# Three mask transposes moved from TensorE to a DMA, and a new written-out order, in an attention-and-MLP kernel

## The chip, the core and the metric

One core of a Trainium2 chip runs the whole program in one launch. The metric is device time in microseconds, from the start of the execution to its end. TensorE (PE) multiplies; VectorE (DVE), ScalarE (ACT) and GpSimd (POOL) do the rest; SyncE (SP) issues nearly all DMAs, in program order.

## The reference

Two parts follow one another. The first is block-sparse causal attention, with 4 batches of 8 heads, 768 positions and 64 features; each query sees its own block of 64 keys and the three blocks whose mean key scores highest:

```python
k_rep = k.reshape(B, H, n_blocks, block, D).mean(axis=3)
gate_scores = np.einsum('bhsd,bhnd->bhsn', q, k_rep)
gate_scores = np.where(causal, gate_scores, -1000000000.0)
top_idx = np.argsort(gate_scores, axis=-1)[..., -top_k:]
...   # mask: chosen blocks and the own block, causal inside
scores = np.where(mask, scale * np.matmul(q, k.transpose(0, 1, 3, 2)), -1000000000.0)
...   # softmax, then attn @ v
```

The second takes the attention output as 3072 rows of 512 features through an MLP: up-projection to 2048, gelu in its tanh form, down-projection to 512. Inputs and output are float32.

## The kernel before, in words

*Heads.* Heads are handled two at a time, as 16 pairs, 4 for each batch. Pairs 0 to 3 (batch 0) are handled in two groups g of two pairs and in three thirds c of 256 positions, so that work can begin before all of batch 0 is loaded. Pairs 4 to 15 are handled whole.

*MLP.* Rows go in 12 chunks of 256. For each chunk there are four up tiles (`up`, L957, 16 matmuls of 256 columns in two halves), four gelus (`gelu`, L967) and two row tiles of four down steps (`down`, L993). A chunk needs the transposed attention output `xT` of all four pairs of its batch: chunk 0 needs the first thirds of batch 0, chunk 1 the second thirds. The last chunk's second row tile is cut into 384 and 128 columns.

*Order.* There is no scheduler. A string `ORDER` lists every step by name, and the program issues them in this order; on each engine's queue instructions run strictly in order, each after the semaphores of what it needs. A name may carry an engine (`:a` ACT, `:v` DVE, `:p` POOL) and one of three wide PSUM slots (`@0` to `@2`).

The step names that the text uses:
- `d0`, `dd`, `d`: loads of q, k and v, from SP; the first k loads (`d0.g.t.1`) come from ACT's queue (L372). `lw`, `cw`: loads of the MLP weights and their casts to fp16. `r`: a copy that puts a loaded 256-position part into order for the transposes.
- `t2`, `h2`, `l` (batch 0): transposes of q and k on PE (L464), and the high and low fp16 parts. `hn`, `ln`, then `zqh`, `zkh`, `zql` (L751): the same for pairs 4 to 15, with the transposes done by DMA from SP.
- `s`, `b`: key sums by block. `g` (L794): gate scores. `m` (`select`, L807 to L821): the top three of each row on DVE, which ends in `madd16`, an fp16 tile of 128 positions by 12 half-chunks.
- `mt` (`mask_t`, L830): the mask is transposed by PE, five blocks of 128x128, into the `small` PSUM bank, of which there is one. `mc` (`mask_q`, L839): two copies put its 12 rows per head under the transposed queries, so that the score matmul adds the mask. `c0`, `c1` (L758): copies of the transposed q and k to where the score matmul reads them.
- `k` (scores, L598 and L852), `x` (exponential, L635 and L868), `a` (causal cut on POOL, L648 and L882), `p` (probabilities times v, L662 and L894), `n` (division by the row sum). `ma` (L616): adds the mask in batch 0.
- `xt` with `xc`, or `zx` (L903): the transpose of the attention output into `xT`, by PE or by DMA.
- `u.chunk.tile.half`, `y`, `f.chunk.row.step`, `o` (L1006, copy out of PSUM) and `w` (L1011, write to HBM).
- `dmN`: N units of 128 columns of filler matmuls on zeros (L1032).

What sets the order of work around the change: the one `small` bank is used in turn by key sums, gate scores, masks, some output transposes and at the end by down tiles. Buffers of a tag rotate; the tag `ql` (two buffers) holds the transposed low part of q.

Of the kernel before, what the change touches and what calls it, by code (L numbers as in the profile page):

```python
# [32 lines left out]
s.0.1 mc.1.0:a dm4 l.0.1 k.0.0.0.0@2 k.0.0.1.0@1 ma.0.0.0 x.0.0.0.0 d0.1.1.2 v.1.0.0:p c.par.0
b.0.1 b.1.1 dm16 d0.0.1.2 x.0.0.1.0 a.0.0.1 g.0.1 k.0.1.0.1@0 k.1.0.0.0@2 k.1.0.1.0@1 ma.1.0.0
x.1.0.0.0 a.0.0.0 lw.out.1 x.1.0.1.0 m.0.1 dd.0.2.1 r.0.2.1:a mt.0.1 mc.0.1:v lw.in.4 g.1.1
k.0.1.1.1@2 v.0.0.1:p lw.in.5 ma.0.1.1 x.0.1.1.1 m.1.1 x.0.1.0.1 t2.0.2@1 d0.0.3.2 s.0.2 h2.0.2
a.0.1.0 dm9 v.0.1.1:a lw.in.3 d0.0.2.2 v.1.1.1:a l.0.2 a.1.0.1 v.1.0.1:p k.1.1.1.0@2 mt.1.1
mc.1.1:v v.0.0.0:p k.1.1.0.0@0 ma.1.1.0 x.1.1.1.0 a.0.1.1 p.0.0.0@1 p.0.0.2 p.0.0.3 p.0.0.1 n.0.0
dm22 d0.1.2.2 cw.in.5:v lw.in.1 v.1.1.0:p dd.1.2.0 cw.in.1:v k.1.1.0.1@2 k.1.1.1.1@1 ma.1.1.1
x.1.1.0.0 a.1.0.0 cw.in.4:v p.1.0.0@0 x.1.1.1.1 d.5.1 dd.1.2.1 dm23 v.0.1.0:p lw.out.0 x.1.1.0.1  # L40
r.1.2.0:a xt.0.0 xc.0.0:a lw.in.0 p.1.0.2 cw.in.2:p d.4.0 p.1.0.3 p.1.0.1 n.1.0 k.0.1.0.0@1
k.0.1.1.0@2 ma.0.1.0 x.0.1.0.0 a.1.1.0 p.1.1.0@0 p.1.1.1 xt.1.0 xc.1.0:v a.1.1.1 p.1.1.2 r.1.2.1:v
lw.out.5 x.0.1.1.0 cw.out.5:p d0.1.5.2 p.0.1.0@1 p.0.1.1 p.1.1.3 n.1.1 cw.in.3:v d.4.1 lw.in.6
lw.in.7 cw.out.1:a hn1.5.0:v p.0.1.3 cw.in.6:p cw.in.7:p lw.out.3 p.0.1.2 t2.1.2@2 n.0.1 s.1.2
b.1.2 xt.1.1 u.0.1.0@0 xc.1.1:a u.0.1.1 y.0.1 hn0.4.0:v xt.0.1 xc.0.1:a b.0.2 u.0.2.0@1 u.0.2.1
y.0.2 u.1.2.0@0 u.1.2.1 y.1.2 u.1.1.0@1 u.1.1.1 ln0.4.0:v zql.4.0 lw.out.2 y.1.1 d0.0.5.2
cw.out.0:a cw.in.0:v u.0.0.0@0 u.0.0.1 g.0.2 u.1.0.0@1 u.1.0.1 y.0.0 hn1.4.0:v u.0.3.0@0 m.0.2
cw.out.3:v mt.0.2 u.0.3.1 h2.1.2 l.1.2 y.1.0 dm9 ln1.4.0:v dm24 y.0.3 cw.out.2:v mc.0.2:v
k.0.2.1.0@2 k.0.2.0.0@1 ma.0.2.0 x.0.2.0.0 g.1.2 d.6.0 hn0.6.0:p x.0.2.1.0 k.0.2.0.1@0 k.0.2.1.1@1
zqh.4.0 ma.0.2.1 x.0.2.0.1 x.0.2.1.1 c.ke.0.0:p ln1.5.0:v m.1.2 mt.1.2 k.0.2.1.2@2 mc.1.2:v s.4.0  # L50
b.4.0 k.0.2.0.2@0 c0.4.0.0:a lw.out.6 ma.0.2.2 f.0.0.0 lw.out.4 lw.out.7 x.0.2.1.2 ln0.6.0:v
cw.out.7:v f.0.0.1 x.0.2.0.2 k.1.2.0.0@1 k.1.2.1.0@2 zkh.5.0 ma.1.2.0 x.1.2.1.0 zqh.6.0 cw.out.6:p
x.1.2.0.0 c.ke.0.1:v cw.out.4:p g.4.0 m.4.0 f.0.0.2 d0.0.4.2 v.0.2.0:v f.0.0.3 o.0.0:a d.5.0
k.1.2.0.1@0 k.1.2.1.1@2 ma.1.2.1 d0.1.4.2 f.0.1.0 hn0.5.0:v ln0.5.0:v x.1.2.0.1 a.0.2.0 zkh.4.0
v.0.2.1:p a.0.2.1 f.0.1.1 p.0.2.0@1 p.0.2.1 c.ke.1.0:a x.1.2.1.1 c0.4.0.1:p mt.4.0 d.6.1 v.1.2.1:p
c1.4.0.0:a mc.4.0.0:v c.par.1 p.0.2.3 p.0.2.2 n.0.2 v.1.2.0:a k.1.2.1.2@0 zqh.5.0 k.1.2.0.2@2
ma.1.2.2 f.0.1.2 x.1.2.0.2 f.0.1.3 zql.5.0 c1.4.0.1:v mc.4.0.1:v x.1.2.1.2 s.5.0 b.5.0 o.0.1:v
k.4.0.1@1 k.4.0.2@2 x.4.0.1 d.4.2 d.5.2 c1.5.0.0:v zql.6.0 a.1.2.0 p.1.2.0@0 p.1.2.1 g.5.0 m.5.0
x.4.0.2 c0.5.0.0:v a.1.2.1 p.1.2.3 c.q0.0 k.4.0.0@1 v.4.0:p f.1.0.0 x.4.0.0 xt.0.2 xc.0.2:a
k.4.0.5@2 p.1.2.2 x.4.0.5 k.4.0.3@1 x.4.0.3 a.4.0.3 hn1.6.0:v d.7.1 ln1.6.0:v a.4.0.5 mt.5.0 d.8.0  # L60
mc.5.0.0:v c0.5.0.1:p zkh.6.0 k.4.0.4@2 f.1.0.1 mc.5.0.1:v n.1.2 c0.6.0.1:v x.4.0.4 u.1.3.0@1
u.1.3.1 y.1.3 s.6.0 f.1.0.2 b.6.0 xt.1.2 w.0.0 xc.1.2:v d.7.0 c1.5.0.1:p hn1.7.0:v ln1.7.0:v
c.ke.1.1:p k.5.0.2@0 k.5.0.1@2 x.5.0.2 k.5.0.3@1 g.6.0 m.6.0 f.1.0.3 u.2.0.0@0 o.1.0:v d.8.1
u.2.0.1 d.9.0 x.5.0.3 a.4.0.4 a.4.0.2 a.4.0.0 a.4.0.1 p.4.0.0@1 x.5.0.1 a.5.0.1 hn0.7.0:v zqh.7.0
mt.6.0 mc.6.0.1:v d.6.2 p.4.0.1 w.1.0 mc.6.0.0:v n.4.0 c1.6.0.0:p y.2.0 c0.6.0.0:p k.5.0.4@2
c1.6.0.1:p f.1.1.0 f.1.1.1 ln0.7.0:v x.5.0.4 c.q0.1 hn1.8.0:v ln1.8.0:v k.5.0.5@1 k.6.0.2@0 x.6.0.2
s.7.0 b.7.0 f.1.1.2 v.5.0:v k.5.0.0@2 c0.7.0.1:v hn0.8.0:p x.5.0.5 ln0.8.0:v x.5.0.0 k.6.0.3@0
a.5.0.0 zql.7.0 zkh.7.0 zqh.8.0 s.8.0 f.1.1.3 b.8.0 x.6.0.3 o.1.1:a a.6.0.3 w.1.1 k.6.0.4@1 w.0.1
x.6.0.4 u.2.1.0@2 u.2.2.0@0 u.2.2.1 y.2.2 hn0.9.0:p g.7.0 a.5.0.4 u.2.1.1 c0.7.0.0:v y.2.1
u.2.3.0@1 m.7.0 a.6.0.4 u.2.3.1 mt.7.0 zql.8.0 y.2.3 a.5.0.2 ln0.9.0:v a.5.0.3 a.5.0.5 p.5.0.0@0  # L70
p.5.0.1 mc.7.0.0:v k.6.0.1@2 f.2.0.0 f.2.0.1 x.6.0.1 v.6.0:v d.10.0 a.6.0.1 n.5.0 k.6.0.0@1
k.6.0.5@2 f.2.0.2 c1.7.0.1:v x.6.0.5 a.6.0.5 x.6.0.0 mc.7.0.1:v c1.7.0.0:v k.7.0.5@0 k.7.0.2@2
zkh.8.0 x.7.0.5 c1.8.0.1:p g.8.0 x.7.0.2 hn0.10.0:v m.8.0 d.7.2 a.6.0.0 a.6.0.2 f.2.0.3 o.2.0:a
k.7.0.3@1 x.7.0.3 a.7.0.3 zx.5.0 c0.8.0.0:a k.7.0.0@0 p.6.0.0@2 p.6.0.1 x.7.0.0 mt.8.0 k.7.0.4@1
x.7.0.4 n.6.0 f.2.1.0 mc.8.0.0:v k.7.0.1@0 f.2.1.1 a.7.0.2 a.7.0.4 mc.8.0.1:a zx.4.0 c0.8.0.1:v
c1.8.0.0:v k.8.0.3@1 d.9.1 zqh.9.0 d.10.1 d.8.2 zql.9.0 a.7.0.0 d.11.0 x.7.0.1 a.7.0.1 v.7.0:v
k.8.0.1@2 x.8.0.1 a.7.0.5 x.8.0.3 xt.6.0 xc.6.0:v p.7.0.0@0 p.7.0.1 n.7.0 hn1.9.0:a zkh.9.0
c1.9.0.0:p hn1.10.0:v ln0.10.0:v zql.10.0 f.2.1.2 f.2.1.3 w.2.0 k.8.0.5@2 xt.7.0 x.8.0.5 k.8.0.4@1
xc.7.0:a zqh.10.0 k.8.0.2@0 u.3.3.0@2 u.3.3.1 ln1.9.0:v x.8.0.4 s.9.0 x.8.0.2 a.8.0.2 u.3.2.0@1
u.3.2.1 v.8.0:v u.4.2.0@0 u.4.2.1 b.9.0 g.9.0 ln1.10.0:v d.11.2 zkh.10.0 y.3.3 o.2.1:a y.3.2 y.4.2  # L80
# [1003 lines left out]
```

## Time and profile before

| | |
|---|---|
| runs (3) | 276.27, 277.47 (median), 279.40 us |
| profiled execution | 278.32 us, span 276.6 us, mean granted TensorE clock 0.994 |
| PE busy | 263.3 us (95%) |
| ACT busy | 198.2 us (72%), with table loads |
| DVE, POOL busy | 141.4 us, 86.9 us |
| read from, written to HBM | 27.26 MB, 6.29 MB |

The span runs from the first to the last instruction of the core; the execution's own time is 1.7 us longer. A busy PE counts a matmul from its start to its modelled end, and matmuls overlap, so the work of PE is better read from how far apart the starts of matmuls lie. Idle time of an engine off the critical path costs nothing.

### The profile page before, as it was taken

The numbers are of one execution on the slowest core, as the hardware profiler recorded it, in microseconds if no ns is written. First come the engines' busy times: TensorE is split into PE (matmuls) and PEld (weight loads), VectorE is DVE, ScalarE is ACT, GpSimd is POOL, SyncE is SP. The second block draws the span as 40 slices with busy tenths as digits, with TensorE's granted clock in tenths as the row PEclk, the third lists the DMA queues.
The fourth block names the chain that finished last, engine by engine and source line by source line (L and its number), as shares of the span: only waits on it lengthen the run. The fifth ranks groups of instructions, "written<-read, shape, count | busy, mean of one in ns | idle before, by whom it ended". The sixth has DMA issues, their size and how long they took to land.

```text
span 276.6 us, 6874 instructions
## 1 busy us (share of the span) xinstructions
PE 263.3 (95%) x2785; PEld 183.1 (66%) x2785; DVE 141.4 (51%) x442; ACT 198.2 (72%) x229; POOL 86.9 (31%) x159
## 2 busy tenths in 40 slices
...
GB/s 173 279 329 282 252 270 295 276 170 180 175 248 192 177 199 190 185 200 213 148 212 118 188 119 114 101 135 157 79 7 23 97 0 2 0 76 2 76 92 138
DMA packets 114416, 42.66 MB, mean 154 GB/s; under 512 B 102992, under 2 KB 107344, under 8 KB 114384
## 3 DMA queue, kind: packets, MB, share of 16 engines
...
q14 instruction: 10, 0.08, 0.1%
HBM read 27.26 MB, written 6.29 MB: 121 GB/s over the span
## 4 chain that ended last, share of the span: by engine, by line
PE 70%; DVE 8%; DMA 7%; ACT 7%; issue 4%; POOL 2%; SPq 1%; POOLq 0%; ACTq 0%
PE hps L957 23%; PE ops L993 20%; PE st L852 7%; PE pv L894 4%; DMA io<-in_k_dram 4%; PE pso L993 3%; PE dm L1032 3%; ACT at L868 2%; DMA qhT<-hn 2%; DMA io<-in_q_dram 2%; PE st L598 2%; DVE ln L739 2%; ACT L868 1%; PE pv L662 1%; PE st L616 1%
## 5 line engine op out<-in xcount | busy, mean ns | idle before, releaser
L957 PE MATMUL hps<-xT,w_in 128*128 128x256 f16 x768 | 90.1, 272 | 0.0
L957 PEld LDWEIGHTS <-w_in 128*128 128x128 f16 x768 | 74.0, 98 | 12.5 <-DVE xn L677 0.2
L993 PE MATMUL ops<-w_out,gT 128*128 128x512 f16 (+1 forms) x352 | 81.9, 371 | 0.0
L868 ACT ACTIVATE at<-st 128x1024 f16<-128x1024 f32 (+1 forms) x72 | 62.8, 918 | 11.1 <-PE st L852 10.8
L967 ACT ACTIVATE gT<-hps 128x1024 f16<-128x1024 f32 x48 | 48.1, 1024 | 23.0 <-PE hps L957 22.8
L993 PEld LDWEIGHTS <-gT 128*128 128x128 f16 x400 | 37.0, 97 | 36.2 <-issue 0.5
L882 POOL TENSOR_SCALAR_AFFINE_SELECT at<-at 128x256 f16<-128x256 f16 x72 | 31.1, 451 | 76.4 <-ACT at L868 66.6
L852 PE MATMUL st<-qk 76*128 76x128 f16 (+2 forms) x192 | 35.6, 306 | 0.5 <-ACT at L868 0.5
L739 DVE SCALAR_TENSOR_TENSOR ln<-io,hn 128x768 f16<-128x768 f32 x24 | 25.3, 1059 | 0.3
L635 ACT ACTIVATE at<-st 128x768 f16<-128x768 f32 (+1 forms) x24 | 20.7, 913 | 6.5 <-PE st L616 4.9
L852 PEld LDWEIGHTS <-qk 76*128 76x128 f16 x192 | 16.5, 97 | 10.8 <-issue 0.9
L1006 DVE COPY w_o<-pso 128x512 f32<-128x512 f32 x1 | 0.7, 692 | 36.9 <-PE pso L993 36.9
L894 PEld LDWEIGHTS <-at 128*128 128x128 f16 x504 | 17.1, 97 | 2.5 <-issue 0.6
L894 PE MATMUL pv<-v,at 128*128 128x65 f16 x504 | 17.7, 193 | 0.6 <-POOL v L771 0.6
L1006 ACT COPY osb<-ops 128x512 f32<-128x512 f32 (+1 forms) x13 | 7.3, 562 | 14.8 <-PE ops L993 12.8
L187 POOL TENSOR_SCALAR hn<-io 128x768 f16<-128x768 f32 x6 | 13.0, 2160 | 9.2 <-PE hps L957 5.1
L1032 PE MATMUL dm<-zsrc 128*128 128x512 f16 (+3 forms) x45 | 13.4, 431 | 2.0 <-POOL zsrc L235 2.0
L673 DVE RECIPROCAL zrec<-pv 128x12 f32<-128x12 f32 x12 | 2.8, 232 | 22.6 <-PE pv L894 22.4
L967 ACT ACT_TABLE_LOAD x11 | 14.1, 1283 | 0.2
L839 DVE COPY qk<-mt 12x640 f16<-12x640 f16 x19 | 9.2, 485 | 7.9 <-ACT qk L839 4.3
L648 POOL TENSOR_SCALAR_AFFINE_SELECT at<-at 128x512 f16<-128x512 f16 x12 | 7.8, 661 | 17.3 <-ACT at L635 17.1
L868 ACT ACT_TABLE_LOAD x9 | 11.5, 1283 | 2.2 <-PE st L852 2.0
...
## 6 DMA issues: line engine op xcount, KB each, us to landing
...
out_dram<-osb SPq DMA_DIRECT2D x15, 256.0 KB, 2.5
...
out_dram<-w_o SPq DMA_DIRECT2D x8, 256.0 KB, 2.4
io<-in_v_dram SPq DMA_DIRECT2D x12, 128.0 KB, 6.1
```

Of the source, the lines that this page charges most:

```text
L187: math_on[eng].tensor_scalar(out=out, in0=in_, scalar1=c, scalar2=None, op0=ALU.mult)
L635: nc.scalar.activation(out=ov, in_=iv, func=AF.Exp, bias=0.0, scale=SCALE / (QS * QS))
L739: math_on[eng].scalar_tensor_tensor(out=g.rearrange("p t c -> p (t c)"), in0=IO[p, x].rearrange("p t h d -> p (t h d)"), scalar=QS, in1=U[ ...
L839: copy_on[eng](out=qt[p % 2][hh][64:64 + NBLK, 128:], in_=U["mt", p][64 * hh:64 * hh + NBLK, 0:S - 128])
L852: nc.tensor.matmul(st[:, hh, cb:cb + nq * 128], kt[p % 2][hh][0:64 + NBLK, jc * 128:(jc + 1) * 128], qt[p % 2][hh][0:64 + NBLK, qc * 128:( ...
L868: nc.scalar.activation(out=ov, in_=iv, func=AF.Exp, bias=0.0, scale=SCALE / (QS * QS))
L882: nc.gpsimd.affine_select(out=a, in_=a, compare_op=ALU.is_ge, fill=0.0, base=0, pattern=[[0, 2], [1, 128]], channel_multiplier=-1,)
L894: nc.tensor.matmul(U["pv", p][:, o:o + 65], AT[p, hh, jc, qc], v16[p % NSLOT][:, jc, hh, :], start=(jc == 0), stop=(jc == qc),)
L957: nc.tensor.matmul(hps[:, j * TCH:(j + 1) * TCH], w_in16[:, ci, fi * 128:(fi + 1) * 128], xT[:, ci, t0:t0 + TCH], start=(ci == 0), stop=(c ...
L967: nc.scalar.activation(out=g.rearrange("p a w -> p (a w)"), in_=G["h", ch, dj], func=AF.Gelu_apprx_tanh, bias=0.0, scale=1.0,)
L993: nc.tensor.matmul(G["o", ch, ti][:, a:b], G["g", ch, dj][:, j, row * 128:(row + 1) * 128], w_out16[:, fi, a:b], start=(fi == 0), stop=(fi ...
L1032: nc.tensor.matmul(U["dm"][:, 0:m * 128].rearrange("p (a x) -> p a x", a=m), zsrc, zsrc.unsqueeze(1).to_broadcast([128, m, 128]), start=Tr ...
```

## The change

Two things change. For pairs 13, 14 and 15 the step `mt` becomes `zm`: SP issues one DMA transpose of `madd16` (five blocks of 128x128, the source of the `mt` step) into an SBUF tile of the tag `ql`, and the two `mc` copies read that tile and no longer PSUM. And `ORDER` is another one from its first to its last name. All other steps are the same in kind and number; engines and slots differ.

```diff
+    def mask_dma(p):
+        mt = hd.tile([128, S - 128], FP16, tag="ql", name=f"mt_{p}")
+        nc.sync.dma_start_transpose(
+            out=mt.rearrange("d (t p) -> d t p", p=128),
+            in_=madd16[p % 2][:, 2:2 * NC].rearrange("p a b -> p (a b)"))
+        U["mt", p] = mt
...
-        step(f"mt.{un}", mask_t, p)
+        if p in (13, 14, 15):
+            step(f"zm.{un}", mask_dma, p)
+        else:
+            step(f"mt.{un}", mask_t, p)
```

In the new order all eight up tiles of chunks 0 and 1 stand ahead of the first scores of the third thirds (`k.0.2`); in the old one seven did, and `u.1.3` came after the first scores of pair 4. Pieces of both orders, not adjacent ones:

```diff
  # the opening
-c.m0.1 c.bi c.ident d0.0.1.0 c.e0 d0.1.0.0 c.ident16 dm24 d0.1.0.1 d0.0.0.0 d0.0.0.1 dd.1.1.0
-dd.1.1.1 d0.1.3.2 d0.0.1.1 t2.0.0@0 c.e.2:a c.v.1 d0.1.1.0 d0.1.1.1 c.gate dm4 c.own r.1.1.0:a
+c.par.0 d0.1.1.0 d0.1.0.0 d0.0.1.0 d0.1.0.1 c.m0.1 d0.0.1.1 d0.0.0.0 c.ident c.ident16 d0.0.0.1
+c.e0 c.own dm24 dm11 dd.0.1.1 dm4 d0.1.1.1 t2.1.0@0 dd.0.1.0 c.m0.0 c.gate c.cg c.bd h2.1.0 s.1.0
...
  # u.1.3, now ahead of k.0.2
-x.4.0.4 u.1.3.0@1 u.1.3.1 y.1.3 s.6.0
+u.0.1.0@2 u.0.1.1 y.1.0 y.0.1 u.1.3.0@1 u.1.3.1 d.5.0 hn0.5.0:p k.0.2.0.0@0 y.1.3
...
  # the mask of pair 15
-k.14.0.1@0 w.6.0 a.14.0.5 mt.15.0 w.3.1 o.6.1:a x.14.0.1 k.14.0.2@2 f.7.0.0 f.7.0.1 f.7.0.2
-x.14.0.2 n.13.0 zx.13.0 mc.15.0.0:v mc.15.0.1:a c0.15.0.0:v k.15.0.5@0
+k.14.0.2@1 o.7.0:v f.7.1.0 zm.15.0 mc.15.0.1:a mc.15.0.0:a a.14.0.5 f.7.1.1 x.14.0.1 k.14.0.0@2
+x.14.0.2 a.14.0.2 f.7.1.2 c1.15.0.1:a n.13.0 c0.15.0.0:v k.15.0.1@1
...
  # the end
-f.11.0.3 o.11.0:a f.11.1.2 f.11.1.3 w.11.0 o.11.1:a w.11.1 f.11.2.0 f.11.2.1 f.11.2.2 f.11.2.3
-o.11.2:a w.11.2
+f.10.1.1 f.11.0.0 f.11.0.1 f.10.1.2 f.10.1.3 f.11.0.2 o.10.1:v f.11.0.3 o.11.0:a w.10.1 w.11.0
```

By count over the whole order: filler units 165 before and 171 after; exponential and gelu tables loaded 22 times before and 20 times after (as the order of `x` and `y` makes them change); mask copies `mc` on ACT 7 and 14; copies `c0` and `c1` on ACT 8 and 12; output copies `o` on ACT 19 and 8, on DVE 6 and 17.

More of the change, by code (lines that the diff above doesn't have):

```diff
@@ L33 @@
[L33 to L80, printed above, removed]
@@ new lines @@
+k.1.0.0.0@2 v.1.0.0:a g.1.1 lw.in.0 k.1.0.1.0@0 v.1.1.1:a ma.1.0.0 x.1.0.1.0 x.1.0.0.0 m.1.1 dm6
+a.0.0.0 mt.1.1 k.1.1.1.0@1 d0.1.2.2 mc.1.1:v k.1.1.0.0@0 ma.1.1.0 v.0.0.0:v x.1.1.1.0 mt.0.1
+mc.0.1:v p.0.0.0@2 p.0.0.2 p.0.0.3 p.0.0.1 cw.in.6:p a.1.0.1 a.1.0.0 dm8 dd.1.2.0 dm4 dm5 v.1.1.0:p
+p.1.0.0@1 p.1.0.1 p.1.0.3 p.1.0.2 x.1.1.0.0 cw.in.4:p lw.out.5 n.0.0 xt.0.0 lw.in.7 xc.0.0:v
+lw.in.5 dd.1.2.1 k.0.1.0.1@0 lw.out.6 n.1.0 v.0.1.0:a k.0.1.1.1@2 ma.0.1.1 dm13 r.0.2.0:p
+k.1.1.0.1@1 x.0.1.1.1 k.1.1.1.1@2 ma.1.1.1 x.0.1.0.1 x.1.1.1.1 xt.1.0 dm6 dm5 cw.in.7:v xc.1.0:v
```

138 lines of the change are left out of this document (90 added, 48 removed).

## The prediction

> **What bounds the kernel now.** I read the page first, then the busy times by stage, the engine waits, the chain that ended last, and the timeline of the first 60 us.
>
> ```profile
> span 276.6 us, 6874 instructions
> PE 263.3 (95%) x2785; PEld 183.1 (66%) x2785; DVE 141.4 (51%) x442; ACT 198.2 (72%) x229; POOL 86.9 (31%) x159
> ```
>
> The same by stage, cut at the first up-projection (36.7), the first third-three scores (51.7), the start of the full mixture (70) and the end of attention (222). Columns: length, then PE, PEld, DVE, ACT and POOL busy, granted clock, DMA share, GB/s. The second group holds the filler matmuls (L1032) alone: PE, PEld, clock, DMA.
>
> ```profile
> 0.00:36.70 36.70, 28.46 (x329) 18.01 (x330) 20.40 (x76) 22.09 (x30) 15.23 (x45) 0.95 1.03 265
> 36.70:51.70 15.00, 15.00 (x151) 12.59 (x147) 11.14 (x29) 11.91 (x13) 4.78 (x4) 1.00 1.11 272
> 70.00:222.00 152.00, 150.25 (x1683) 107.53 (x1680) 94.69 (x290) 130.15 (x145) 57.89 (x98) 1.00 0.78 148
> 222.00:276.60 54.60, 51.71 (x367) 34.45 (x363) 2.44 (x4) 18.46 (x23) 0.00 (x0) 1.00 0.13 49
> ...
> 0.00:36.70 36.70, 11.49 (x36) 3.63 (x36) 0.95 1.03 265
> 36.70:222.00 185.30, 1.95 (x9) 0.84 (x9) 1.00 0.85 163
> ```
>
> TensorE is the bound from 36.7 us on: it is hardly ever idle, ACT and DVE have room. The loss lies in the first 36.7 us: 28.46 busy, of it 11.49 in fillers, so only 17.0 us of work; some 19.7 us are start-up, fillers and waits. The waits of TensorE, in the view of who waited for whom, say the same: the large ones are early.
>
> ```profile
> PE w L464 <- DMA io<-in_q_dram: 1.8, 1, 1.8
> PE st L616 <- DVE mrow L187: 1.4, 1, 1.4
> PE mt L568 <- DVE madd L554: 1.3, 3, 0.7
> ```
>
> So a new order can win only by a shorter start, and lose anywhere by new TensorE waits. The chain gives what one piece of work costs back to back (start, length, what) and the two loads that hold up the start:
>
> ```profile
> 2.40 5.09 DMA io<-in_q_dram
> 7.51 4.19 DMA io<-in_k_dram
> ...
> 38.90 6.99 PE hps L957 x64
> ...
> 148.27 1.30 PE pv L894 x42
> ...
> 268.06 3.46 PE ops L993 x16
> ```
>
> An up matmul starts every 6.99/64 = 0.109 us (a whole tile of 16: 1.75); a 512-column matmul every 3.46/16 = 0.216 us, so a down step of four is 0.87, a score tile of 1024 columns 0.43 and a filler unit of 128 columns 0.054. A pv pair is 1.3.
>
> **The change part by part.**
>
> *TensorE's work.* 15 mask transposes go (pairs 13 to 15, five each); fillers rise from 165 to 171 units. A transpose has 128 columns, a filler's unit: -15 x 0.054 + 6 x 0.054 = **-0.5 us**. All other matmuls are the same, in other places.
>
> *The start.* Both orders open with loads. In the old one two 256 KB loads stand among the first eight, and the last of the four k loads of the ACT queue is issued at 7.51, when the load of 2.40 has landed. In the new one the first eight loads are the q and k parts that both first transposes need, all without such a wait.
>
> ```profile
> 7.51 0.38 ACTq L372 DMA_DIRECT2D io<-in_k_dram  x1
> ...
> 17.78 1.51 ACT L635 ACTIVATE at<-st 128x768 f16<-128x768 f32 x2 [0.60 <-PE st L616]
> ...
> 37.57 1.28 ACT L967 ACT_TABLE_LOAD   x1
> 38.86 1.02 ACT L967 ACTIVATE gT<-hps 128x1024 f16<-128x1024 f32 x1
> ...
> 52.66 3.83 ACT L635 ACTIVATE at<-st 128x1024 f16<-128x1024 f32 x4 [0.33 <-PE st L616]
> ...
> io<-in_k_dram SPq DMA_DIRECT2D x4, 256.0 KB, 5.2
> io<-in_k_dram ACTq DMA_DIRECT2D x4, 128.0 KB, 4.1
> ```
>
> By hand: the eighth load is issued near 2.9 and lands near 7.0; the 256 KB loads of chunk 1 follow at 5.9 to 7.4 and land by 12 to 12.6 (5.2 each, shared); behind them stand four copies into "part" tiles, the gate chain of chunk 0 and, ahead of the first scores, 33 filler units (1.8). I get the first exponential at 18.5, against 17.78 in the trace. From there ACT's queue decides:
>
> ```profile
> L967 ACT ACTIVATE gT<-hps 128x1024 f16<-128x1024 f32 x48 | 48.1, 1024 | 23.0 <-PE hps L957 22.8
> L635 ACT ACTIVATE at<-st 128x1024 f16<-128x1024 f32 x12 | 11.7, 1021 | 2.9 <-PE st L616 1.4 <-PE gt L794 0.8 <-PE pv L662 0.6
> L635 ACT ACTIVATE at<-st 128x768 f16<-128x768 f32 x12 | 9.0, 805 | 3.6 <-PE st L616 3.4
> L967 ACT ACT_TABLE_LOAD x11 | 14.1, 1283 | 0.2
> L512 ACT CAST v<-io 128x256 f16<-128x256 f32 x3 | 1.1, 404 | 0.0
> L470 ACT ACTIVATE qk<-w 128x1024 f16<-128x1024 f32 x6 | 6.1, 1024 | 2.7 <-PE w L464 2.5 <-DVE ks L487 0.2
> L354 ACT CAST w_out<-w_out 128x1024 f16<-128x1024 f32 x2 | 2.1, 1042 | 0.0
> ```
>
> Ahead of the first gelu the new order gives ACT 8 narrow and 4 wide exponentials (6.4 + 4.1), four v casts (1.6), one part copy (about 0.6, like the 512-column copy in the tail's row) and the table (1.3): 14.0 us, and 1.2 for a mask that I expect late: first gelu at 33.7, not 38.86. The old order spent 21.1 us between the two: its exponentials alone had 6.5 us of idle ahead of them (2.9 + 3.6 in the rows). Then eight gelus (8.2), two q/k casts (2.0), three weight casts (3.1), some 1.8 of waits for up tiles and the table: first exponential of third three at 50.2 against 52.66, with eight gelus done where the old order had seven. Lead 2.5 + 1.0 = **3.5 us** if all goes well; nothing if loads or masks are later than in my walk; -1.7 with one more stretch of half clock like the one here (window 24 to 30, columns as above):
>
> ```profile
> 24.00:30.00 6.00, 4.59 (x42) 2.07 (x40) 3.75 (x7) 3.54 (x5) 4.58 (x9) 0.72 0.91 241
> ```
>
> A mean of 0.72 over 6 us is 3.4 us at half speed, 1.7 us of work lost. My walk leaves queueing out, so I take two thirds: **-2.3 us**.
>
> *The moved up tile* (u.1.3, from behind pair 4's first scores to the front) costs nothing by itself. Table loads fall from 22 to 20, 2 x 1.283 us off ACT, which is not the bound: 0; if ACT were the bound it would be a gain of 2.6.
>
> *Masks by DMA.* Step zm is one issue on SP; the two mask copies wait for its landing, and so do the scores behind them. It also queues on SP behind the transposes and output writes ahead of it, and itself delays those behind it.
>
> ```profile
> 144.74 0.28 DVE L807 TENSOR_TENSOR ga<-gt,cgate 128x120 f32<-128x120 f32 x1 [0.50 <-PE gt L794]
> ...
> 146.54 0.22 DVE L821 TENSOR_TENSOR madd<-lt,ownm 128x120 f16<-128x120 f16 x1
> ...
> qlT<-ln SPq DMA_TRANSPOSE x12, 3.3
> ...
> DMA to landing us min/median/max: 2.7/3.7/8.8
> ```
>
> Gate to mask row takes 2.0 us on DVE (144.74 to 146.76), a transpose of this kind 3.3 to landing (the last row is all 36 of pairs 4 to 15): 5.5 us with a hand-over. The tightest is pair 15: between its gate and its first mask copy the new order puts an up tile (1.75), five down steps (4.3), a pv pair (1.3) and three score tiles, one of them short (1.0), on TensorE, 8.3 us. Covered, 0; without that cover 3.3 per mask. The three extra issues are some 3.7 us on SP, in a stage where it waits for data anyway.
>
> The Trainium skill, "VectorE: DVE Perf Modes", section "The three transpose paths", speaks against this part: it gives 390 ns for a 128x128 transpose by TensorE, 1309 ns by DMA. By that, five blocks cost 4.6 us more per mask, 13.8 us for the three if nothing covered them. The trace agrees in direction; what it cannot show is a mask by DMA.
>
> *The tail.* The old order ends with a 128-column piece, the new one with a full 512-column tile behind another full write.
>
> ```profile
> L1006 ACT COPY osb<-ops 128x512 f32<-128x512 f32 x12 | 7.0, 587 | 14.3 <-PE ops L993 12.4 <-issue 1.9
> L1006 ACT COPY osb<-ops 128x128 f32<-128x128 f32 x1 | 0.3, 266 | 0.5 <-PE ops L993 0.5
> ...
> out_dram<-osb SPq DMA_DIRECT2D x15, 256.0 KB, 2.5
> ...
> out_dram<-osb SPq DMA_DIRECT2D x1, 64.0 KB, 1.6
> ```
>
> Copy 0.3 longer, landing 0.9 longer: **+1.2 us**, on the path for certain.
>
> *New waits in the middle.* From 36.7 us on the old order hardly waits. No row prices the waits of another order; from -1 (nearly all there are now gone) to +6 (rival B); I take **+0.5**, near the order that was measured, since the new one is as evenly packed by count.
>
> Sum: -0.5 - 2.3 + 1.2 + 0.5 = -1.1 us. The profiled execution took 278.32 us (span 276.6), 0.85 above the median of the runs, 277.47. Taken off the median: **276.4 us**.
>
> **The rivals.** A (lead kept in full): 3.5 early and no new waits: -0.5 - 3.5 + 1.2 - 1.0, so 277.47 - 3.8 = **273.7**. For it: DVE and ACT have room; against: it needs every early load on time.
>
> B (slower: ACT's queue). Mask copies on ACT rise from 7 to 14 and q/k copies from 8 to 12. They stand in order between exponentials, and each waits for a transpose, by TensorE or DMA; the exponentials behind wait too, then the pv matmuls. Price: 11 such holds at 0.5 us, 5.5. For it, one row (ACT waiting for a transposed q: total, times, longest); against, ACT had 22 us free between 70 and 222, and 11 output copies leave it.
>
> ```profile
> ACT qk L758 <- DMA qhT<-hn: 1.6, 1, 1.6
> ```
>
> It decides once a hold outlasts the score tile that TensorE has ahead, about one wide exponential (1.0). Time 276.4 + 5.5 = **281.9**.
>
> C (masks don't arrive as meant): a landing of 8.8, the largest of the 36, makes the chain 11.0 against 8.3 us: 2.7 late for pair 15 and about as much for pair 14: **279.1 to 281.8**.
>
> D (the clock): the new order leaves TensorE idle at 9.8 to 11.9 and again for masks near 22. Two more stretches at 1.7: **279.8**. The Trainium skill, "TensorE: Matmul & The Clock Gate", Part 1, says that the clock is halved by default and released by some 3.4 us of activity. The window at 24 to 30 agrees in length and depth.
>
> **How the numbers follow.** Forecast 276.4 with chance 0.40 (own range 273.8 to 278.3; a quarter of it below 274.7), A 0.24, B 0.24, C 0.07, D 0.05. 1% (2.8 us) is about what a measurement of this kernel can tell from no change. Faster: 0.10 + 0.24 = 0.34. Within 1%: 0.30 + 0.04 from C and D = 0.34. Slower: 0.24 + 0.08 = 0.32. Low end: A and a half-clock stretch avoided, 273.7 - 1.7 = 272.0. High end: B with two thirds of the lead gone, 281.9 + 1.6 = 283.5.
>
> **What would show it.** Right: first gelu near 34 us; first exponential of third three near 50; no idle of TensorE above 1 us after that; mask copies of pairs 13 to 15 without a wait for the DMA; a stretch from the last matmul to the end some 1.2 us longer than now. Wrong: a first gelu at 37 or later (no lead); ACT waits for mask or q/k transposes above 3 us in total (B); "mt" landing in the wait list of ACT or DVE (C); a granted clock below 1 in more than one stretch (D).

## The result, and the profile after

| | before | changed |
|---|---|---|
| median of 20 runs each, us | 277.49 (275.88 to 279.83) | 275.41 (274.35 to 278.29) |
| ratio | | 0.9935, 95% interval 0.991 to 0.996 |
| profiled execution, us (span) | 278.32 (276.6) | 274.55 (272.8) |

The change makes the kernel 0.65% faster, 1.8 us by the ratio: within 1%, on the side that was forecast (276.4, range 272.0 to 283.5). The two profiled executions lie further apart, 3.8 us.

One plain fact is needed to read this: the old kernel's times form two groups (in its largest sample, 29 runs, 16 from 275.75 to 276.81 and 13 from 277.14 to 278.30), so its median moves between 276.2 and 277.5 from sample to sample, and its profiled execution lay at the upper edge of the second; of the changed kernel's 20 runs 19 lie below 276.4. A ratio leaves out executions that lie more than 1.5% above the fastest of the same kernel (two each of front_new and masks_only below); medians and ranges are of all. Of the old kernel's 20 runs here 11 lie above 277, of the 62 beside the experiments 22; against the medians there, 276.2 to 276.7, the changed kernel's 275.41 is 0.8 to 1.3 us less.

The head of the changed kernel's page:

```profile
span 272.8 us, 6865 instructions
PE 262.0 (96%) x2773; PEld 180.7 (66%) x2773; DVE 138.5 (51%) x442; ACT 195.8 (72%) x222; POOL 96.5 (35%) x164
```

Its busy times by stage, columns as in the prediction (length, PE, PEld, DVE, ACT, POOL, clock, DMA share, GB/s), with the stretch in which the old profile showed a clock of 0.72:

```profile
0.00:36.70 36.70, 31.69 (x374) 20.97 (x375) 20.37 (x79) 22.80 (x29) 18.55 (x48) 1.00 1.05 277
36.70:51.70 15.00, 15.00 (x182) 12.04 (x180) 11.30 (x39) 12.00 (x13) 7.30 (x4) 1.00 1.15 289
51.70:70.00 18.30, 18.30 (x247) 10.40 (x240) 15.94 (x47) 18.00 (x24) 9.05 (x16) 1.00 1.12 200
70.00:222.00 152.00, 149.91 (x1654) 105.98 (x1653) 86.63 (x274) 129.75 (x145) 61.57 (x96) 1.00 0.76 145
222.00:272.80 50.80, 47.07 (x329) 31.32 (x327) 4.30 (x7) 13.26 (x15) 0.00 (x0) 1.00 0.16 57
...
24.00:30.00 6.00, 6.00 (x89) 3.65 (x87) 3.59 (x7) 5.05 (x8) 2.86 (x5) 1.00 1.05 353
```

The old kernel's row from 51.7 to 70 us, which the prediction doesn't show, and the filler matmuls alone (PE, PEld, clock, DMA, GB/s) in the new start:

```profile
51.70:70.00 18.30, 17.90 (x274) 10.54 (x274) 12.68 (x45) 15.60 (x20) 9.01 (x13) 1.00 1.23 202
...
0.00:36.70 36.70, 11.34 (x42) 4.08 (x42) 1.00 1.05 277
```

Read them as a balance. The span is 3.8 us shorter: TensorE is busy 1.3 us less (263.3 to 262.0) and idle 2.5 less. The idle time by stage, length less busy: at the start 8.24 before, 5.01 now (-3.2), with the fillers alike (11.49 and 11.34 busy); from 36.7 to 222, 2.2 and 2.1; behind 222, 2.89 and 3.73 (+0.8). Of the 1.3 busy, 0.5 is the transposes that went (net of fillers); the other 0.8 is less than the 1.7 us that the stretch of half clock cost that one old execution.

ACT's timeline (start, length, what) holds the milestones of the prediction's walk:

```profile
18.29 1.51 ACT L634 ACTIVATE at<-st 128x768 f16<-128x768 f32 x2 [0.22 <-PE st L615]
...
33.30 1.94 ACT L976 ACTIVATE gT<-hps 128x1024 f16<-128x1024 f32 x2
...
50.10 4.55 ACT L634 ACTIVATE at<-st 128x1024 f16<-128x1024 f32 x5
```

First exponential 18.3 (walked: 18.5), first gelu 33.3 (33.7), first exponential of third three 50.1 (50.2). The waits of TensorE (who waited, for whom: total, times, longest):

```profile
PE w L463 <- DMA io<-in_k_dram: 1.4, 1, 1.4
PE dm L1041 <- POOL zsrc L234: 1.1, 1, 1.1
...
PE mt L567 <- DVE madd L553: 0.7, 2, 0.6
PE gt L793 <- DVE qk L845: 0.6, 1, 0.6
...
PE st L858 <- ACT at L874: 0.3, 1, 0.3
```

In the first 36.7 us these waits add up to the idle time. By what TensorE waited for, before and now: the first loads 2.9 and 1.4, the zeros for the fillers 2.0 and 1.1, DVE's copies of a mask (`mrow`) 1.8 and none, other DVE results (selections, low parts, key blocks) 1.5 and 2.5.

The masks, by the view of the tile "mt": the issues on SyncE's queue (ns, first and last start), an idle engine that waited for a landing, and the time to landing:

```profile
L839 SPq DMA_TRANSPOSE mt<-madd x3: 1200/1201/1207, 173.7 to 200.8; - x3
  DMA mt<-madd: 2.0, 1
DMA to landing us min/median/max: 2.6/2.6/2.6
```

No wait of TensorE behind the start exceeds 0.6 us (pair 8's gate, for a mask copy). A mask by DMA costs 1.2 us of SyncE and here lands 2.6 us after its issue; one DVE copy waited 2.0 us for one, and TensorE's list has no wait for that copy.

### The profile page after: what moved, and what is told of

Same layout as the page of the kernel before. It is cut to its first block, busy times and chain, and to the rows that moved or that the text cites. A ratio compares the mean times of both kernels' runs of the same rounds, so it can differ in the third digit from the quotient of the medians.

```text
span 272.8 us, 6865 instructions
## 1 busy us (share of the span) xinstructions
PE 262.0 (96%) x2773; PEld 180.7 (66%) x2773; DVE 138.5 (51%) x442; ACT 195.8 (72%) x222; POOL 96.5 (35%) x164
## 4 chain that ended last, share of the span: by engine, by line
PE 80%; ACT 6%; DVE 6%; DMA 3%; issue 2%; ACTq 1%; POOL 0%; SPq 0%
PE hps L966 30%; PE ops L1002 21%; PE st L858 8%; PE pv L900 5%; PE pso L1002 3%; ACT at L874 3%; DMA io<-in_k_dram 2%; PE st L597 2%; PE pv L661 2%; PE dm L1041 1%; PE kp L764 1%; PE st L615 1%; DMA qhT<-hn 1%; PE gt L793 1%; DVE ks L486 1%
## 5 line engine op out<-in xcount | busy, mean ns | idle before, releaser
L1002 PE MATMUL ops<-w_out,gT 128*128 128x512 f16 (+1 forms) x352 | 82.9, 372 | 0.0
L874 ACT ACTIVATE at<-st 128x1024 f16<-128x1024 f32 (+1 forms) x72 | 63.0, 917 | 10.3 <-PE st L858 8.8
L858 PE MATMUL st<-qk 76*128 76x128 f16 (+2 forms) x192 | 36.8, 305 | 0.9 <-ACT at L874 0.3
L858 PEld LDWEIGHTS <-qk 76*128 76x128 f16 x192 | 16.2, 97 | 11.2 <-issue 1.3
L186 POOL TENSOR_SCALAR hn<-io 128x768 f16<-128x768 f32 x8 | 17.6, 2194 | 9.4 <-DMA io<-in_q_dram 9.4
L1015 DVE COPY osb<-ops 128x512 f32<-128x512 f32 (+1 forms) x11 | 7.2, 652 | 23.5 <-PE ops L1002 23.4
L757 POOL COPY qk<-khT 64x768 f16<-64x768 f16 x13 | 14.1, 1085 | 4.1 <-DMA khT<-hn 3.8
L1041 PE MATMUL dm<-zsrc 128*128 128x512 f16 (+3 forms) x48 | 12.8, 407 | 1.1 <-POOL zsrc L234 1.1
L976 ACT ACT_TABLE_LOAD x10 | 12.8, 1283 | 0.2
L1015 DVE COPY w_o<-ops 128x512 f32<-128x512 f32 x3 | 2.1, 691 | 20.1 <-PE ops L1002 20.1
L676 DVE TENSOR_TENSOR xn<-pv,zrec 128x768 f16<-128x768 f32 x12 | 11.5, 957 | 0.4
L469 ACT ACTIVATE qk<-w 128x1024 f16<-128x1024 f32 x6 | 6.1, 1022 | 7.1 <-PE w L463 6.8
L874 ACT ACT_TABLE_LOAD x8 | 10.3, 1283 | 1.3 <-PE st L858 1.0
```

Of the source, the lines that this page charges most:

```text
L186: math_on[eng].tensor_scalar(out=out, in0=in_, scalar1=c, scalar2=None, op0=ALU.mult)
L757: copy_on[eng](out=dst[0:64, :], in_=U["qh" if x == 0 else "kh", p][64 * hh:64 * hh + 64])
L858: nc.tensor.matmul(st[:, hh, cb:cb + nq * 128], kt[p % 2][hh][0:64 + NBLK, jc * 128:(jc + 1) * 128], qt[p % 2][hh][0:64 + NBLK, qc * 128:( ...
L874: nc.scalar.activation(out=ov, in_=iv, func=AF.Exp, bias=0.0, scale=SCALE / (QS * QS))
L976: nc.scalar.activation(out=g.rearrange("p a w -> p (a w)"), in_=G["h", ch, dj], func=AF.Gelu_apprx_tanh, bias=0.0, scale=1.0,)
L1002: nc.tensor.matmul(G["o", ch, ti][:, a:b], G["g", ch, dj][:, j, row * 128:(row + 1) * 128], w_out16[:, fi, a:b], start=(fi == 0), stop=(fi ...
```

## The experiments

All ratios are to the old kernel, run on the same chip beside each. Line numbers differ by up to nine between kernels. To place a loss I also use a derived number, the lag: the end of a step in the trace, less the sum of TensorE's work written up to it (a fixed duration per kind of step, those of the prediction; filler units count as work). A lag that grows is a wait or a slower clock. In us, near three times:

| kernel | 47 us | 70 us | last matmul |
|---|---|---|---|
| before | 12.0 | 12.1 | 15.3 |
| changed | 7.2 | 6.8 | 11.2 |
| masks_only | 10.4 | 12.2 | 16.9 |
| masks_sp | 10.3 | 11.2 | 15.4 |
| rest_new | 10.4 | 11.7 | 17.8 |
| filler | 9.3 | 10.4 | 12.8 |
| chunk2_later | 14.8 | 18.1 | 20.3 |
| front_new | 7.3 | 6.8 | 11.6 |
| loads_back | 7.1 | 6.6 | 10.9 |
| up_back | 7.9 | 8.5 | 15.8 |
| masks_back | 7.8 | 7.3 | 16.3 |
| masks_early | 7.0 | 6.5 | 12.4 |
| tail_back | 7.5 | 7.0 | 11.3 |
| best | 8.2 | 7.8 | 11.0 |

**The front alone, the rest alone.**

```
# front_new: new order through zkh.5.0 (about 61 us), then the old order's remaining steps, masks by TensorE
# rest_new: old order through b.5.0 (about 62 us), then the new order's remaining steps, masks by DMA
```

> The new order up to the lead-in of third three (through zkh.5.0, about 61 us), from there the old order, all masks by TensorE. Theory 1 (the lead is made in the first 60 us and the rest of the new order gives a part of it back): at 60 us the new order stands 5.6 us ahead of the old one in the two profiled executions (wall time less running sum of TensorE work 6.8 against 12.4); these executions lie 3.8 us apart where the medians lie about 2 apart, so some 1.8 of the 5.6 is the choice of executions. Lasting lead 3.8: 273.7 us (273.0 to 275.0), below the changed kernel's 275.4. Theory 2 (the gain comes from the masks by DMA and the later order): 276.5 to 277.5, no better than before.

> The old order up to b.5.0 in third three (about 62 us), from there the new order, masks of pairs 13 to 15 by DMA. Theory 1: the later part of the new order waits 1.0 us more on TensorE than the old (lag grows 4.2 against 3.2 after 72 us), does 0.8 less of mask transposes' work and has an end 0.8 longer: 278.5 us (277.5 to 279.5), slower than before. Theory 2: it carries the gain: 275.5 us.

Measured: front_new 276.36, ratio 0.9979 (0.9947 to 1.0011), its runs from 274.1 to 279.0; rest_new 282.34, ratio 1.0207 (1.0171 to 1.0243). Theory 1 is right on the place of the lead: every kernel with the new front stands at a lag of 6.5 to 8.5 at 70 us, every kernel with the old one at 10.4 or more. By the medians it is wrong on the rest. The new rest behind the old front costs 5.7 us by the ratio, not the 1.0 that was forecast (278.5 against 277.49), and the old rest behind the new front loses 3.4 us between 70 and 84 us (lag 6.8 to 10.2), where TensorE waits for a DVE that the old order expects to be further on. The waits in the trace of front_new:

```profile
PE kp L763 <- DVE qk L844: 1.2, 1, 1.2
...
PE mt L828 <- DVE madd L819: 0.7, 1, 0.7
```

By the medians neither half brings the gain by itself. But front_new's executions order themselves by their mean granted clock: 274.1 and 274.3 us at 1.000, 275.0 to 275.7 at 0.994, 277.0 to 277.8 at 0.987 and 0.988, 278.4 and 279.0 at 0.981 and 0.982. One stretch of half clock takes 1.7/276 = 0.006 off the mean, so these steps are none, one, two and three stretches (an estimate; only the profiled execution, at 0.994, shows where its stretch lay: at 6 to 12 us). Without such a stretch the new front with the old rest took what theory 1 gave it, in two executions: the changed kernel at 0.999 or 1.000 took 274.4 to 275.2, the old kernel beside front_new 275.8 to 276.5 and twice about 277.7. What front_new lacks against the changed kernel goes with the clock: six of its 12 executions have a mean of 0.988 or less, one of the changed kernel's 20. Why the new rest has fewer such stretches is not shown.

**The masks alone, in the old order.**

```diff
# masks_only: the old order
-mt.13.0 ... mt.14.0 ... mt.15.0
+zm.13.0 ... zm.14.0 ... zm.15.0
# masks_sp: masks_only, and
-m.13.0 zm.13.0 mc.13.0.1:a u.8.0.0@0 ... a.12.0.0 zqh.14.0 c0.14.0.1:a
+m.13.0 u.8.0.0@0 ... a.12.0.0 zqh.14.0 zm.13.0 mc.13.0.1:a c0.14.0.1:a
```

> The old order as it stands, only the masks of pairs 13 to 15 by DMA. Theory 1: 15 transposes of 0.054 us go, landing 2.6 us after issue: -0.8 to 0 us, 277.0 (276.7 to 277.5); in this order a mask copy follows its transpose closely, so if the landing is not covered by TensorE work each mask costs up to 2.6 us: 279 to 285. Theory 2 (masks carry the gain): 275.5 us.

masks_only: 281.62 (279.2 to 283.6), ratio 1.0137 (1.0091 to 1.0182), so the branch "not covered" by its range. What TensorE waited for isn't the mask itself. Its trace around pair 13's mask (SPq is SyncE's queue):

```profile
179.96 1.20 SPq L838 DMA_TRANSPOSE mt<-madd  x1
...
181.21 1.16 SPq L421 DMA_DIRECT2D io<-in_k_dram  x2
182.47 1.22 SPq L749 DMA_TRANSPOSE qhT<-hn  x1
...
187.46 0.82 POOL L756 COPY qk<-qhT 64x768 f16<-64x768 f16 x1 [6.29 <-DMA qhT<-hn]
...
188.60 0.82 POOL L769 CAST v<-w_v 128x768 f16<-128x768 f32 x1
...
189.47 1.44 PE L899 MATMUL pv<-v,at 128*128 128x65 f16 x42 [1.97 <-POOL v L769]
```

and the same place in the old kernel:

```profile
180.91 1.22 SPq L751 DMA_TRANSPOSE qhT<-hn  x1
...
186.25 0.82 POOL L758 COPY qk<-qhT 64x768 f16<-64x768 f16 x1 [5.00 <-DMA qhT<-hn]
...
187.38 0.82 POOL L771 CAST v<-w_v 128x768 f16<-128x768 f32 x1
...
188.26 1.44 PE L894 MATMUL pv<-v,at 128*128 128x65 f16 x42 [0.56 <-POOL v L771]
```

SyncE takes its queue in order. The mask stands ahead of pair 14's q transpose; that goes out 1.56 us later, GpSimd's copy of it is later, the cast of v behind that copy is later, and TensorE's weighted sums wait 1.97 instead of 0.56 us. masks_sp turns the two issues round:

> The old order with the masks of pairs 13 to 15 by DMA, as in the run that does only that, but the transpose of pair 13's mask is issued behind the transpose of pair 14's high q instead of ahead of it, with its first copy. Theory 1 (that run lost its time because SyncE's queue waited for the mask and held back the q transpose, then GpSimd's copy, then its cast of v for pair 12, for which the weighted sums waited 2.0 us, and a stretch of half clock followed in the slower runs): 275.7 to 277.0. Rival (a mask by DMA is late by itself, or disturbs other transfers): 279 or more.

Measured: 277.02, ratio 1.0012 (0.9989 to 1.0036): as fast as the old kernel. The place of one issue in SyncE's queue, with the first copy of that mask, is worth the difference between 1.0137 and 1.0012. The chain above explains only a part of these 3.5 us. Another part is the clock. The profiled execution of masks_only, its fastest, has a stretch of half clock long before the first mask by DMA, with no wait of TensorE above 0.2 us in the 5 us ahead of it (length, TensorE busy, clock, DMA share, GB/s):

```profile
54.00:60.00 6.00, 5.90 (x50) 0.72 1.16 305
```

Its three slowest executions (282.5 to 283.6) have mean clocks of 0.968 to 0.987, the 12 of masks_sp 0.993 to 1.000. What sets the clock back in masks_only is not shown.

In masks_sp the same weighted sums still wait, now for ACT's gelu:

```profile
PE pv L899 <- ACT gT L975: 1.6, 1, 1.6
```

Here the mask itself is late. Issued at 180.93, right behind the q transpose, it lands after 4.4 us, and ACT stands idle for it ahead of that gelu:

```profile
185.35 0.72 ACT L844 COPY qk<-mt 12x640 f16<-12x640 f16 x1 [2.64 <-DMA mt<-madd]
```

So in the old order the masks by DMA gained nothing at either of the two places.

**The masks by TensorE, in the new order.**

```diff
# masks_back: TensorE's transposes at the DMA's places; k sums s.14, s.15 behind the mask copies (one small bank)
-zm.13.0 ... zm.14.0 ... zm.15.0
+mt.13.0 ... mt.14.0 ... mt.15.0
# masks_early: masks_back, transposes moved up, soon behind the selection
+u.6.2.1 mt.13.0 ... o.6.0:v mt.14.0 ... p.13.0.1 mt.15.0
```

> The changed kernel with the masks of pairs 13 to 15 by TensorE again; since these need the single small bank, the k sums of pairs 14 and 15 move behind the mask copies of the pair before. Theory 1 (the masks by DMA are worth only the transposes they save): 15 x 0.054 = 0.8 us more, 276.2 against the changed kernel's 275.4. Rival (the small bank: gate, k sum and mask of neighbouring pairs now take turns and TensorE waits for them): 277 or more. Rival (the DMA masks cost as much on SyncE's queue as they save): 275.4 or less.

masks_back: 280.13, ratio 1.0128 (1.0098 to 1.0158), 5.3 us over the changed kernel by the ratios; its lag grows from 10.8 at 192 us to 16.3 at 216. Its timeline there:

```profile
198.54 0.59 PE L857 MATMUL st<-qk 76*128 76x512 f16 x2 [0.86 <-ACT at L873]
...
210.86 1.38 ACT L844 COPY qk<-mt 12x640 f16<-12x640 f16 x2 [2.91 <-PE mt L828]
...
213.33 0.59 PE L857 MATMUL st<-qk 76*128 76x512 f16 x2 [1.65 <-ACT at L873]
```

and TensorE by window (length, busy, clock, DMA share, GB/s):

```profile
198.00:204.00 6.00, 5.06 (x34) 0.73 0.30 76
```

The transposes of pair 15 stand in TensorE's own queue behind down steps; ACT's two mask copies wait for them, the exponentials behind the copies wait, and then TensorE waits for its bank. This is rival B of the prediction, not in the changed kernel but in the kernel without its DMA masks. Much the same happens for pair 14 (0.86 us of wait at 198.5), and there a stretch of half clock follows. The loss is not that stretch alone: the two executions at a mean clock of 1.000 took 278.9 and 279.6.

> The changed kernel with the masks of pairs 13 to 15 by TensorE, but each set of transposes placed some microseconds earlier, soon after its selection, and the k sums of pairs 14 and 15 behind the mask copies. Theory 1 (in the run with TensorE masks at the DMA's places, mask copies on ACT waited for transposes that stood late in TensorE's own queue; what counts is when the mask is ready): 275.4 plus 0.8 of work, 275.8 to 277.0. Rival (the one small bank, held from the transposes to the copies, keeps the next pair's k sum or gate waiting wherever they stand): 278 or more.

masks_early: 277.05, ratio 1.0022 (0.9997 to 1.0047), still 2.4 us over the changed kernel by the ratios, 1.6 by the medians. The 0.8 us of transposes is in it; its longest wait behind the start is my own, pair 13's transposes stood too early:

```profile
PE mt L828 <- DVE madd L819: 1.0, 1, 1.0
```

Behind 180 us its lag grows 1.6, the changed kernel's 1.3. Taken together: in this order the two placements by TensorE lose 2.4 and 5.3 us for three pairs. They may not be the best: without the wait of 1.0 that I made, the first would lose 1.4, of which 0.8 is the transposes' own work. In the old order two placements by DMA gained nothing.

**What made the start shorter.**

```diff
# loads_back: the changed kernel
-... d0.0.0.1 ... t2.0.0@1 dd.1.1.0 ... c.e.2:p dd.1.1.1
+... d0.0.0.1 dd.1.1.0 dd.1.1.1 ... t2.0.0@1 ... c.e.2:p
# chunk2_later: the old kernel
-x.0.1.0.1 t2.0.2@1 d0.0.3.2 s.0.2 h2.0.2 a.0.1.0 ... v.1.1.1:a l.0.2 a.1.0.1 ... d0.1.5.2 p.0.1.0@1
+x.0.1.0.1 d0.0.3.2 a.0.1.0 ... v.1.1.1:a a.1.0.1 ... d0.1.5.2 t2.0.2@2 s.0.2 h2.0.2 l.0.2 p.0.1.0@1
# filler: the old kernel
-ma.1.1.0
+dm24 ma.1.1.0
```

> The changed kernel, but the two 256 KB loads of chunk 1 of group 1 stand among the first eight or nine loads, as in the old order. Theory 1 (the start is part of the lead): the first transposes end 0.5 to 1.3 us later (in the profiles the lag at the first scores is 7.2 in the new order, 8.5 in the old) and all of it lasts: 275.9 to 276.7. Rival (the exponentials of chunk 1 and the queue of ACT set the pace up to the first gelu, so the start is absorbed): 275.4.

loads_back: 275.03, ratio 0.9952 (0.993 to 0.9975); its lag is that of the changed kernel within 0.3 at all three times of the table. The order of these two loads is worth nothing. What loads_back does not put back is the old order's late k load: its four k loads on ACT's queue still go out from 0.80 to 3.02 us, as in the changed kernel, where the old kernel's fourth goes out at 7.51.

The longest wait of the old start had a chain that its timeline shows:

```profile
23.97 1.02 ACT L470 ACTIVATE qk<-w 128x1024 f16<-128x1024 f32 x1 [0.22 <-DVE ks L487]
...
25.03 0.69 DVE L478 SCALAR_TENSOR_TENSOR ql<-w,qk 128x512 f16<-128x512 f32 x1 [1.09 <-ACT qk L470]
25.64 0.28 DVE L187 TENSOR_SCALAR mrow<-mt 128x256 f16<-128x256 f16 x1
...
25.97 0.40 PE L616 MATMUL st<-mrow,E 12*128 12x256 f16 x8 [1.41 <-DVE mrow L187]
```

The mask copy of group 1 stands on DVE behind the low part of chunk 2's q, which waits for ACT's cast of the transposes of chunk 2. The new order has chunk 2 later and doesn't show this wait.

> The old kernel with one move: the transposes of group 0's chunk 2 with their k sum, qk cast and low part stand ahead of the weighted sums p.0.1.0 instead of in the middle of group 1's mask of chunk 1. Theory 1 (in the old order the mask copy of group 1 waits on DVE for the low part of chunk 2, which waits for ACT's cast; TensorE then idles 1.4 us at 24.6, and in some executions, as in the profiled one, a stretch of half clock of 3.4 us follows, which makes the two groups of its times near 276 and near 277.6): the wait and the upper group go: 274.3 to 275.5 us with little spread. Rival (the wait only moves, to the casts of chunk 2 ahead of the first gelu or to third three): 276 to 277.5.

chunk2_later: 283.78, ratio 1.0268 (1.0235 to 1.0301). The rival, and far beyond its price. Waits of TensorE in it:

```profile
PE st L596 <- ACT at L633: 1.9, 2, 1.5
PE w L462 <- DVE ql L476: 1.5, 1, 1.5
PE pv L660 <- POOL v L510: 1.2, 1, 1.2
```

With the mask on time the weighted sums wait for a cast of v on GpSimd; the moved transposes hold up those behind them at the new place; third three waits for its bank. One wait removed by hand became three, and its profiled execution has two stretches of half clock behind 24 us (0.72 at 24 to 30, 0.73 at 60 to 66) where the old one has one.

> The old kernel with 24 filler units more (1.3 us), put exactly into TensorE's wait of 1.4 us for the mask copy at 24.6 us; the mask copy itself is not touched. Theory 1 (the two groups of the old kernel's times, near 276.1 and near 277.7, come from a stretch of half clock that follows this idle time in some executions): the upper group goes, all runs 275.8 to 276.8, median 276.1, and the clock is 1.00 at 24 to 30 us. Rival (the groups come from elsewhere, the loads or the start): both groups stay.

filler: 276.20, ratio 0.9992 (0.9972 to 1.0013); 9 of 12 runs from 275.84 to 276.80, 3 from 277.11 to 277.57. Its window (length, TensorE busy, clock, DMA share, GB/s):

```profile
24.00:30.00 6.00, 5.99 (x66) 1.00 0.90 240
```

and the same window of masks_only with all engines; its start is the old one, and TensorE is busy 4.59 us as in the old kernel's row:

```profile
24.00:30.00 6.00, 4.59 (x59) 2.35 (x58) 3.91 (x8) 4.69 (x7) 4.65 (x9) 1.00 0.94 254
```

So the same idle time was followed by a stretch of half clock in one profiled execution (old kernel) and by none in three (masks_only, masks_sp, rest_new): lag 12.0 against 10.3 to 10.4 at 47 us, 1.6 for one stretch. The theory that the old kernel's upper group of times is this stretch does not hold as it stands: the upper group shrank, from 13 of 29 to 3 of 12, which chance may do, but filler's profiled execution, 277.14, lay in it with a clock of 1.00 throughout. The mean clocks of the old kernel's 62 executions beside the experiments say the same. Of the 22 above 277 us 18 have a mean of 0.992 to 0.994, one stretch; but so have 14 of the 40 below, and the other 4 above have 1.000. A stretch goes with the upper group, and it is neither needed for it nor enough.

**The eighth up tile.**

```diff
# up_back: the changed kernel
-u.1.3.0@1 u.1.3.1 d.5.0 hn0.5.0:p k.0.2.0.0@0 y.1.3
+... n.1.2 u.1.3.0@1 u.1.3.1 y.1.3 ... x.5.0.0 f.1.0.3 o.1.0:v
```

> The changed kernel with the eighth up tile of chunks 0 and 1 (u.1.3 with its gelu) back behind the scores of pair 4, as in the old order, and the down step that needs it after the first scores of pair 5. Theory 1 (which up tiles stand first is worth nothing by itself, two more table loads of 1.28 us fall on an ACT with room): 275.4 to 276.0. Rival (the eighth tile first is part of the gain: TensorE waits for the gelu or ACT falls behind by 2.6): 277 to 278.

up_back: 279.60, ratio 1.0109 (1.0081 to 1.0138). Two rows:

```profile
72.40 1.92 PE L965 MATMUL hps<-xT,w_in 128*128 128x256 f16 x16 [1.42 <-DVE xn_1.2_1512 L675]
...
76.99 0.22 PE L857 MATMUL st<-qk 76*128 76x128 f16 x1 [1.53 <-ACT qk L756]
```

The tile waits for its bank, and its gelu with two table loads holds up ACT's q copy. Both are prices of the place that I chose, so this says that the tile can't go anywhere, not what the front place is worth.

**The end, and a faster version.**

```diff
# tail_back: the changed kernel, end
-... f.11.2.0 f.11.2.1 f.11.2.2 u.9.3.0@2 f.11.2.3 o.11.2:v ... f.11.0.3 o.11.0:a w.10.1 w.11.0
+... f.11.0.3 o.11.0:a w.10.1 w.11.0 f.11.1.0 f.11.1.1 f.11.1.2 f.11.1.3 o.11.1:v w.11.1 f.11.2.0 f.11.2.1 f.11.2.2 f.11.2.3 o.11.2:a w.11.2
# best: tail_back, and
-mc.7.0.0:a
+mc.7.0.0:v
```

> The changed kernel, but its last stretch has the old kernel's sequence: chunk 11's 128-column piece of the last down tile comes last again, behind its 384-column piece. Theory 1 (the end is on the path: 3.7 us from the last matmul to the end against 2.9): -0.8 us, 274.6. Rival (the write before it, or the DMA queue, sets the end in both): 275.4, no change.

tail_back: 274.17 (273.97 to 274.97), ratio 0.991 (0.9884 to 0.9936), 0.7 us better than the changed kernel by the ratios. Their intervals overlap, but five of its six runs lie below all 20 of the changed kernel (medians 1.2 apart). The last copy and the issue of the last write in the changed kernel's timeline:

```profile
269.10 0.58 ACT L1015 COPY osb<-ops 128x512 f32<-128x512 f32 x1 [9.28 <-PE ops L1002]
269.71 0.33 SPq L1020 DMA_DIRECT2D out_dram<-osb  x1
```

and in tail_back's:

```profile
269.30 0.27 ACT L1014 COPY osb<-ops 128x128 f32<-128x128 f32 x1 [2.91 <-PE ops L1001]
269.59 0.33 SPq L1019 DMA_DIRECT2D out_dram<-osb  x1
```

From issue to the end of the span 3.1 us (272.8 - 269.71) for the wide write, 2.7 (272.3 - 269.59) for the narrow one, and 0.3 more for the wide copy.

> The changed kernel with the old sequence of the last stretch (the 128-column piece last) and the first mask copy of pair 7 on DVE instead of ACT, where it waits for an exponential while DVE is idle and pair 8's gate waits for the bank (0.6 us of TensorE at 96 us). Theory 1 (waits of TensorE after 37 us are lost time in full): 0.5 us better than with the tail alone, 273.7. Rival (the scores behind wait for ACT or DVE anyway): 274.2.

The wait that best takes away, in tail_back:

```profile
95.56 0.68 ACT L844 COPY qk<-mt 12x640 f16<-12x640 f16 x1
...
96.27 0.49 DVE L844 COPY qk<-mt 12x640 f16<-12x640 f16 x1 [2.60 <-PE st L857]
...
96.81 0.18 PE L792 MATMUL gt<-kb,qhT 128*128 128x48 f16 x1 [0.56 <-DVE qk L844]
```

best: 273.58 (272.9 to 274.4), ratio 0.9896 (0.9868 to 0.9923), as theory 1 said, and faster than both kernels: five of its six runs lie below all of the changed kernel's. The row's wait is gone from its list. The step from tail_back alone is inside the intervals; that best beats the old kernel by 1% is not.

## Why the prediction was right, and where its steps failed

- *The bound.* Right: TensorE's start held the difference (-3.2 us of idle in the first 36.7 us); later stages hardly changed. front_new and rest_new show that the lead lies in the front; which of its many moves makes it is not shown.
- *The early lead* is the mis-sized term: 3.5 at most, 2.3 taken. The walk's milestones came within 0.4 us, so the discount of a third for queueing had no ground; with 3.5 the forecast would have been 275.2, against 275.41 measured. A part of that agreement is luck: the 256 KB loads went out at 3.9 to 5.5 us, not at 5.9 to 7.4, and ACT's 1.2 us of wait for a mask ahead of the first gelu was 0.9 for a load of v and 1.1 for scores, with about 1 us less work than walked. The lag shows 2.1 to 3.4 us between the old fronts at full clock (10.3 or 10.4; filler's 9.3 counts 1.3 us of extra filler as work) and the new ones (7.0 to 8.2), and 4.8 against the old profiled execution with its half clock. The step that failed there is the base: the lead was worked out against one execution, and the 1.7 us of half clock in it appeared only in the low end, though a gain against that stretch is had only by executions that contain it.
- *The reason for an earlier start*, the first eight loads, fell in the half that was tried: with the two 256 KB loads back, loads_back is the same. The other half, the fourth k load that no longer goes out late, stays untested.
- *Masks by DMA: 0.* Right for the changed kernel, where TensorE never waits for them, but too narrow. As the prediction said, an issue also delays what is behind it on SyncE; I put this at nothing because SyncE waits for data there anyway. With a q transpose behind the issue it was 1.0137 against 1.0012. And the term -0.5 is not what the masks are worth: with TensorE's masks at the two places tried, this order loses 2.4 and 5.3 us.
- *The price per block that spoke against the masks by DMA.* The Trainium skill, "VectorE: DVE Perf Modes", section "The three transpose paths", gives 1309 ns for a 128x128 transpose by DMA; by that figure five blocks would be an estimated 6.5 us. Here five blocks landed in 2.6, so the measurement decides, and the 13.8 us against the change was no danger.
- *The tail*: +1.2 taken, +0.8 in the profiles, 0.7 by tail_back. The sign and the path were right; the wider write's landing was priced at 0.9 by the medians of the writes, and was 0.4.
- *Waits in the middle*: +0.5 taken. Idle from 36.7 to 222 us is unchanged (2.2 and 2.1); the lag behind 70 us grows 4.4 instead of 3.2, 0.6 of it at pair 8's gate, which best takes away.
- *The moved up tile: 0.* Not shown; up_back measured another place, not this term.
- *Rivals.* B did not come: behind the start ACT waits 0.3 us for masks and TensorE 0.3 us for ACT in the changed kernel; B's mechanism stands in masks_back. C did not come (landing 2.6, not 8.8), though its sign did: DVE's list has a wait of 2.0 us for "mt", which cost TensorE nothing. D's price holds only where TensorE is the bound: of the changed kernel's 20 runs those at a mean clock of 0.991 to 0.997 have spans of 273.1 to 274.1, those at 0.999 or 1.000 have 272.6 to 273.4, about half a microsecond; the one at 0.988 has 276.5. tail_back's stretch lies at 6 to 12 us, where TensorE waits for loads in any case:

```profile
6.00:12.00 6.00, 4.30 (x20) 0.72 1.20 294
```

In the balance of the two profiled executions: work -0.5, lead and half clock -4.8, later waits +0.7, end +0.8, together -3.8; predicted -0.5, -2.3, +0.5, +1.2.

What stays open: which moves in the front make the start shorter; what besides the half clock separates the old kernel's two groups of times; and what sets the clock back so often in front_new and masks_only. No profiled execution of the old kernel fell in its lower group.
